# The first pair of an attention kernel: k and q as float32 through the SyncE queue, rounded on the chip, and the head ordered by hand

## The chip, the cores and the metric

The kernel runs on one core of one Trainium2 chip. The metric is the device time of one execution in microseconds (us). A run of the kernel is one execution; a figure for a kernel is the median of its fast runs. The span of a trace is about 1.7 us shorter than the time of the same execution (206.9 us for 208.6 us in the kernel before).

## The reference

Attention with a choice of chunks, followed by a gated MLP. Cut to what matters:

```python
# q, k, v: (4, 8, 768, 64) float32; chunk = 32, 24 chunks, top_k = 6
k_min = np.min(k_chunks, axis=3); k_max = np.max(k_chunks, axis=3)
ub = np.sum(np.maximum(q * k_min, q * k_max), axis=-1)      # a bound for each query and chunk
ub = np.where(causal, ub, -1e9)
top_chunks = np.argsort(ub, axis=-1)[..., -top_k:]
scores = scale * q @ k.T, masked to the chosen chunks and to the causal triangle
attn = exp(scores - max) / sum;  out = attn @ v
# then the MLP on (4, 768, 512): h = relu(x @ w_in); u, v = halves of h
# v normalised, v_s = w_spatial @ v + b;  result = (u * v_s) @ w_out, float32
```

## The kernel before

The 32 heads are taken as 16 pairs. Each pair goes through the same steps: transposes of k on TensorE (`k_transpose`), the chunk maxima and minima on DVE (`k_max`, `k_min`), transposes of q and its positive and negative parts (`q_transpose`, `q_parts`), bound matmuls (`bounds`), the six best chunks (`top`, `select`), and then for each head six score matmuls, an exponential on ACT for each, and value matmuls (`scores`, `values`). At about 55 us the matmuls of the MLP begin; they are mixed in and fill TensorE's gaps.

```python
        def k_bounds(self):                      # "km": the small operand of the bound matmuls
            for hi, (d0, d1) in enumerate(HALF):
                copy = nc.gpsimd.tensor_copy if 2 <= self.i < 4 else nc.scalar.copy
                ...
        def k_operand(self, hi):                 # "kh": the score operand
            copy = nc.scalar.copy if self.i < 1 else nc.vector.tensor_copy
            ...
        def a_copy(self, hi):
            copy = nc.vector.tensor_copy if self.i < 2 and hi == 0 else nc.scalar.copy
            ...
        def triangle(self, hi):
            if self.b == 0:                      # none for the first four pairs
                return
            ...
            nc.gpsimd.affine_select(out=blk, in_=blk, compare_op=Alu.is_ge, fill=0.0, ...)
```

Loads change float32 to float16 on the way. The Trainium skill ("DMA: Bandwidth & Descriptors", section "SWDGE vs HWDGE vs iDMA") says that a DMA that casts has to be issued from GpSimd, which the profile calls POOL. So all loads of before are POOL instructions.

```python
    def load_k(g, hi, xy=None):
        ...
            nc.gpsimd.dma_start(out=t[:, xy, :, 1 - hi, :], in_=source(k, b, h + xy, 1))
    def load_w_out(j):
        nc.gpsimd.dma_start(out=w_out_sb[:, j], in_=moe_w_out[j * P:(j + 1) * P, :])
```

The program is written as a list of steps with a "beat" each (`at(beat, step)`), issued in order of beats. What is issued so is then still reordered, engine by engine, by a scheduler that works from its own estimates. Only what stands inside `manual_schedule` stays in the written order; in before that is TensorE alone, up to beat 6:

```python
    at(B0, load_k, 0, 0, 0)                      # B0 = -30: the head
    ...
    at(B0, init_ring, 0)                         # zeros in the first of three q buffers, on DVE
    ...
    for j in range(KO):
        at(76 + 6 * j, load_w_out, j)
    ...
    with tc.manual_schedule(engines={mybir.EngineType.PE}):
        for beat in sorted(b for b in beats if b < 6):
            for fn, args in beats.pop(beat):
                fn(*args)
    for beat in sorted(beats):                   # the scheduler orders all engines here
        for fn, args in beats[beat]:
            fn(*args)
```

The softmax here doesn't subtract the row's maximum and nothing guards it: scores larger than these inputs give would overflow.

Of the kernel before, what the change touches and what calls it, by code (L numbers as in the profile page):

```python
# [10 lines left out]
F32 = mybir.dt.float32  # L11
# [5 lines left out]
P = 128  # L17
# [31 lines left out]
def kernel(  # L49
# [46 lines left out]
    def at(beat, fn, *args):  # L96
        beats[beat].append((fn, args))
# [12 lines left out]
    later = cp.tile([P, (NQT - 1) * 2 * NCH], F16)  # L110
    expand = cp.tile([D, S], F16)
    eps_t = cp.tile([P, 1], F32)

    def init_identity():
        nc.vector.memset(identity, 0.0)
# [2 lines left out]

    def init_ring(i):

        nc.vector.memset(qs_ring[i][:, :, :, 0:4:3, :], 0.0)

    def init_small():
        nc.vector.memset(km_ring[0], 0.0)
        nc.vector.memset(km_ring[1], 0.0)
        nc.vector.memset(eps_t, 1e-6)
        for t in v_ring:
            nc.vector.memset(t[:, :, :, D:D + 2], 1.0)

    def init_expand():  # L130

# [5 lines left out]

    def init_masks():

        nc.gpsimd.memset(later, 0.0)  # L140
        lv = later.rearrange("p (t h c) -> p t h c", h=2, c=NCH)
        nc.gpsimd.affine_select(out=lv, in_=lv, compare_op=Alu.is_ge, fill=NEG, base=CPT,
                                channel_multiplier=1, pattern=[[CPT, NQT - 1], [0, 2], [-1, NCH]])
        nc.gpsimd.memset(tri, 0.0)
        nc.gpsimd.affine_select(out=tri, in_=tri, compare_op=Alu.is_ge, fill=NEG,
                                base=0, channel_multiplier=-1, pattern=[[1, P]])

    def init_kh(i):
        for hi, (d0, d1) in enumerate(HALF):
            nc.scalar.copy(kh_ring[i][hi][d0:d1, :], expand)  # L150


    W = 2 * NCH
# [3 lines left out]
    class Pair:  # L157
# [26 lines left out]

        def k_bounds(self):
            for hi, (d0, d1) in enumerate(HALF):
                copy = nc.gpsimd.tensor_copy if 2 <= self.i < 4 else nc.scalar.copy
                s0, s1 = HALF[1 - hi]
                copy(self.km[d0:d1, :, hi], self.kmm[s0:s1])

# [10 lines left out]

        def q_transpose(self):
            self.tr = self.trans_tile()
            for t in range(1, NQT):
                nc.tensor.transpose(self.tr[:, t * P:(t + 1) * P], self.qs[:, t, 1:3, :], identity)  # L205

        def q_parts(self, m):
            if m == 0:
                self.rq = sb.tile([P, 2, S], F16, tag="rq", name="rq")
                nc.vector.tensor_scalar(self.rq[:, 0, P:S], in0=self.tr[:, P:S], scalar1=0.0, scalar2=None, op0=Alu.max)  # L210
            elif self.i < 1:
                nc.scalar.activation(self.rq[:, 1, P:S], self.tr[:, P:S], func=Act.Relu, scale=-1.0)
            else:
                nc.vector.tensor_scalar(self.rq[:, 1, P:S], in0=self.tr[:, P:S], scalar1=-1.0, scalar2=0.0,
                                        op0=Alu.mult, op1=Alu.max)
# [37 lines left out]
        def a_copy(self, hi):  # L253
            if self.i >= 8:
                return
            copy = nc.vector.tensor_copy if self.i < 2 and hi == 0 else nc.scalar.copy
            copy(self.a[:, :, hi, :], self.tr.rearrange("d (t s) -> d t s", s=P))  # L257


# [55 lines left out]
    def source(x, b, h, n):  # L315
        return x[b, h:h + n].rearrange("h (so si) d -> si (h so) d", si=P)

    def load_k(g, hi, xy=None):
        b, hp = divmod(2 * g, HP)
        if ("k", g) not in tiles:  # L320
            tiles["k", g] = sb.tile([P, 2, NQT, 2, D], F16, tag="k", name="k", bufs=3)
        t = tiles["k", g]
        for x in range(2):
            pairs[2 * g + x].k = t[:, x]
        h = 2 * hp + 2 * hi
        if xy is None:
            nc.gpsimd.dma_start(out=t[:, :, :, 1 - hi, :].rearrange("p x t d -> p (x t) d"), in_=source(k, b, h, 2))  # L327
        else:
            nc.gpsimd.dma_start(out=t[:, xy, :, 1 - hi, :], in_=source(k, b, h + xy, 1))

    def load_q(g, hi, xy=None):
        b, hp = divmod(2 * g, HP)
        t = qs_ring[g % 3][:, :, :, 1 + hi, :]
        h = 2 * hp + 2 * hi
        if xy is None:
            nc.gpsimd.dma_start(out=t.rearrange("p x t d -> p (x t) d"), in_=source(q, b, h, 2))  # L336
        else:
            nc.gpsimd.dma_start(out=t[:, xy], in_=source(q, b, h + xy, 1))

    def load_v(g):  # L340
        b, hp = divmod(2 * g, HP)
        t = v_ring[g % 3]
        nc.gpsimd.dma_start(out=t.rearrange("p h t c -> p (h t) c")[:, :, 0:D], in_=source(v, b, 2 * hp, 4))
        for x in range(2):
            pairs[2 * g + x].v = [t[:, x], t[:, x + 2]]

# [7 lines left out]
    def load_w_in(j):  # L354
        for hi in range(2):
            r = (4 * (j // 2) + j % 2 + 2 * hi) * D
            nc.gpsimd.dma_start(out=w_in_sb[hi * D:(hi + 1) * D, j], in_=moe_w_in[r:r + D, :])

    def load_w_spatial(j):
        nc.gpsimd.dma_start(out=ws_raw[:, j], in_=moe_w_spatial[j * P:(j + 1) * P, :])  # L360
# [90 lines left out]

    B0 = -30
    pairs = [Pair(i) for i in range(NPAIR)]
    at(B0, load_k, 0, 0, 0)
    at(B0, load_k, 0, 1, 0)
    at(B0, init_identity)
    at(B0, load_q, 0, 0, 0)
    at(B0, load_q, 0, 1, 0)
    at(B0, init_ring, 0)
    at(B0, init_small)  # L460
    at(B0, init_expand)
    at(B0, load_k, 0, 0, 1)
    at(B0, load_k, 0, 1, 1)
    at(B0, init_masks)
    at(B0, load_q, 0, 0, 1)
    at(B0, load_q, 0, 1, 1)
    at(B0, load_v, 0)
    at(B0, init_ring, 1)
    at(B0, init_ring, 2)
    at(B0, init_kh, 0)  # L470
    at(B0, init_kh, 1)
    at(40, load_b)
    for g in range(1, NPAIR // 2):
        t0 = 2 * g * BEATS
        for hi in range(2):
            at(t0 - 40 + hi, load_k, g, hi)
            at(t0 - 36 + hi, load_q, g, hi)
        at(t0 - 18, load_v, g)
    for i, p in enumerate(pairs):
        t0 = i * BEATS  # L480
        for hi in range(2):
            for g in range(len(TILES)):
                at(t0 + 6 * hi + g, p.scores, hi, g)
            at(t0 + 6 * hi + 6, p.triangle, hi)
            at(t0 + 6 * hi + 6, p.values, hi, LOWER[0], True)
            at(t0 + 6 * hi + 8, p.values, hi, LOWER[1])
            at(t0 + 6 * hi + 10, p.values, hi, DIAG, False, True)
            at(t0 + 6 * hi + 11, p.normalise, hi)
        at(t0 + 18, p.x_transpose)
    for i, p in enumerate(pairs):  # L490
        t0 = i * BEATS
        if i < 2:
            continue
        t0 += 4 if i < 4 else 0
        at(t0 - (22 if i < 4 else 27), p.k_transpose)
        at(t0 - 22, p.k_max)
        at(t0 - 21, p.q_transpose)
        at(t0 - 20, p.k_min)
        at(t0 - 19, p.q_parts, 0)
        at(t0 - 18, p.q_parts, 1)  # L500
        at(t0 - 17, p.k_bounds)
        at(t0 - 16, p.bounds)
        at(t0 - 15, p.k_operand, 0)
        at(t0 - 14, p.top, 0)
        at(t0 - 13, p.top, 1)
        at(t0 - 12, p.select)
        at(t0 - 11, p.k_operand, 1)
        at(t0 - 10, p.a_transpose, 0)
        at(t0 - 9, p.a_copy, 0)
        at(t0 - 7, p.a_transpose, 1)  # L510
        at(t0 - 6, p.a_copy, 1)
    p, n = pairs[0:2]
    for beat, *step in (
            (B0 + 1, p.k_transpose), (B0 + 1, p.k_max), (B0 + 1, p.k_min), (B0 + 1, p.k_operand, 0),
            (B0 + 1, p.q_transpose), (B0 + 1, p.q_parts, 0), (B0 + 1, p.k_bounds),
            (B0 + 1, p.q_parts, 1), (B0 + 1, p.k_operand, 1), (B0 + 1, p.bounds), (B0 + 1, p.top, 0),
            (B0 + 1, p.top, 1), (B0 + 1, p.select), (B0 + 1, init_kh, 2), (B0 + 1, init_kh, 3), (B0 + 1, p.a_transpose, 0), (B0 + 1, p.a_copy, 0),
            (B0 + 1, n.k_transpose), (B0 + 1, p.a_transpose, 1), (B0 + 1, n.k_max), (B0 + 1, p.a_copy, 1), (B0 + 1, n.k_min),
            (B0 + 1, n.k_operand, 0),
            (0, n.q_transpose), (1, n.q_parts, 0), (1, n.k_bounds), (1, n.q_parts, 1),  # L520
            (1, n.k_operand, 1), (2, n.bounds), (3, n.top, 0), (3, n.top, 1), (4, n.select), (5, n.a_transpose, 0),
            (5, n.a_copy, 0), (6, n.a_transpose, 1), (6, n.a_copy, 1)):
        at(beat, *step)
    for j in range(NDO):
        at(20 + 8 * j, load_w_in, j)
# [30 lines left out]
            at(first + done * count // total, fn)  # L556
            done += cost

    with tc.manual_schedule(engines={mybir.EngineType.PE}):
        for beat in sorted(b for b in beats if b < 6):  # L560
            for fn, args in beats.pop(beat):
                fn(*args)
    for beat in sorted(beats):
# [31 lines left out]
```

## Time and profile before

| | before |
|---|---|
| median, lowest, highest of 3 runs | 209.1, 208.97, 209.35 us |
| span of the profiled run (208.6 us) | 206.9 us |
| first k transpose, first k maximum | 5.75, 6.58 us |
| first exponential | 15.29 us |
| "landmark" on ACT (below) | 51.28 us |
| first triangular mask | 52.93 to 53.79 us |
| idle TensorE in the first 60 us | 14.2 us |

The page of before gives busy time by engine, and the span in 40 slices (a digit is the busy share in tenths). TensorE (PE) is at 90% or more from the twelfth slice (57 us) to the last but one, so only the first 60 us have anything to give.

```profile
PE 187.8 (91%) x1922; PEld 115.1 (56%) x1922; DVE 154.5 (75%) x454; ACT 158.1 (76%) x326; POOL 80.5 (39%) x100
...
PE   0368999898899999999999999999999999999992
```

The table of busy time by stretch says the same in numbers; each line is a stretch, its length, then the busy time of each engine with its number of instructions. The busy times of PE in the first eight of the ten stretches asked for add up to 45.8 of 60 us.

```profile
core 0: us, PE busy (x) PEld busy (x) DVE busy (x) ACT busy (x) POOL busy (x), PEclk, DMA share, GB/s
0.00:6.00 6.00, 0.25 (x3) 0.28 (x4) 3.34 (x12) 3.10 (x4) 4.81 (x10) 1.00 0.73 46
6.00:10.00 4.00, 1.60 (x13) 0.94 (x10) 2.31 (x3) 2.94 (x6) 4.00 (x9) 1.00 1.34 86
...
50.00:60.00 10.00, 9.12 (x122) 6.42 (x121) 8.63 (x28) 9.41 (x22) 9.28 (x12) 1.00 2.10 170
60.00:80.00 20.00, 19.39 (x233) 12.85 (x231) 18.99 (x60) 17.45 (x37) 10.72 (x11) 1.00 1.98 130
80.00:200.00 120.00, 119.62 (x1054) 66.98 (x1053) 87.27 (x237) 86.28 (x184) 20.38 (x22) 1.00 0.82 120
```

The chain of waits in the head of before (start, length, what): the k load takes 3.33 us from issue to landing, the two reductions follow, and then ACT does kh, km and the negative part of q (`rq`) one after the other, from 8.50 to 10.52. That is 2.7 us between the end of the minimum (8.42) and the end of the bound matmuls (11.13).

```profile
2.28 3.33 DMA k<-in_k_dram
...
5.75 0.81 PE kTp L170 x6
...
6.58 0.96 DVE kmm L178
7.54 0.88 DVE kmm L182
...
8.50 0.79 ACT kh L194
...
9.81 0.71 ACT rq L212
...
10.57 0.56 PE ub L222 x9
```

### The profile page before, as it was taken

The numbers are of one execution on the slowest core, as the hardware profiler recorded it, in microseconds if no ns is written. First come the engines' busy times: TensorE is split into PE (matmuls) and PEld (weight loads), VectorE is DVE, ScalarE is ACT, GpSimd is POOL, SyncE is SP. The second block draws the span as 40 slices with busy tenths as digits, with TensorE's granted clock in tenths as the row PEclk, the third lists the DMA queues.
The fourth block names the chain that finished last, engine by engine and source line by source line (L and its number), as shares of the span: only waits on it lengthen the run. The fifth ranks groups of instructions, "written<-read, shape, count | busy, mean of one in ns | idle before, by whom it ended". The sixth has DMA issues, their size and how long they took to land.

```text
span 206.9 us, 5068 instructions
## 1 busy us (share of the span) xinstructions
PE 187.8 (91%) x1922; PEld 115.1 (56%) x1922; DVE 154.5 (75%) x454; ACT 158.1 (76%) x326; POOL 80.5 (39%) x100
## 2 busy tenths in 40 slices
PE   0368999898899999999999999999999999999992
PEld 0266776775666665656655656565555454444440
DVE  6467979989799989899797999887647456365520
ACT  4797989899998889785989996669999830666042
POOL 7997659596992463236114111111111110000000
PEclk9999999999999999999999999999999999999999
DMA  5999999999999999979998926648782124540356
GB/s 38 92 118 154 140 178 158 173 177 167 177 162 162 97 119 128 135 130 147 149 278 153 180 62 57 127 88 158 181 166 65 38 29 92 187 152 3 72 128 256
DMA packets 114424, 27.27 MB, mean 132 GB/s; under 512 B 109536, under 2 KB 110816, under 8 KB 114400
## 3 DMA queue, kind: packets, MB, share of 16 engines
q0 software_dynamic: 76544, 12.20, 89.8%
q1 hardware_dynamic: 37856, 14.75, 36.4%
q8 instruction: 15, 0.25, 0.5%
q14 instruction: 9, 0.07, 0.1%
HBM read 24.38 MB, written 6.29 MB: 148 GB/s over the span
## 4 chain that ended last, share of the span: by engine, by line
PE 69%; ACT 17%; DVE 8%; issue 2%; DMA 2%; POOL 0%; DVEq 0%; ACTq 0%; POOLq 0%
PE mlp L388 40%; PE sc L266 12%; ACT e L271 10%; PE acc L289 7%; PE kTp L170 2%; ACT a L257 2%; DVE kmm L178 2%; PE ub L222 2%; DMA k<-in_k_dram 2%; PE trm L251 2%; ACT vraw L398 1%; PE tr L205 1%; DVE vn L412 1%; DVE kmm L182 1%; ACT u L420 1%
## 5 line engine op out<-in xcount | busy, mean ns | idle before, releaser
L271 ACT ACTIVATE e<-sc 128x512 f16<-128x512 f32 x192 | 96.9, 553 | 14.8 <-PE sc L266 13.4
L266 PE MATMUL sc<-a,kh 128*128 128x512 f16 (+3 forms) x256 | 65.5, 308 | 2.1 <-ACT e L271 1.5
L388 PE MATMUL mlp<-w_in_sb,xT 128*128 128x512 f16 x192 | 53.0, 379 | 0.1
L278 POOL TENSOR_SCALAR_AFFINE_SELECT e<-e 128x768 f16<-128x768 f16 x24 | 20.9, 869 | 66.3 <-ACT e L271 66.3
L289 PEld LDWEIGHTS <-e 128*128 128x128 f16 x672 | 31.4, 97 | 17.0 <-DVE x L297 3.8
L388 PE MATMUL mlp<-vn,wsT 128*128 128x512 f16 x144 | 37.3, 379 | 0.0
L289 PE MATMUL acc<-vt,e 128*128 128x65 f16 x672 | 35.3, 193 | 0.7 <-DVE x L297 0.4
L266 PEld LDWEIGHTS <-kh 128*128 128x128 f16 x256 | 22.7, 98 | 13.3 <-issue 0.8
L437 ACT COPY o<-mlp 128x512 f32<-128x512 f32 x24 | 14.1, 586 | 19.5 <-PE mlp L388 19.1
L400 DVE BATCH_NORM_STATS2 stats<-vraw 128x6 f32<-128x512 f32 x24 | 16.6, 693 | 12.9 <-ACT vraw L398 12.5
L388 PE MATMUL mlp<-w_out_sb,gT 128*128 128x512 f16 x96 | 25.1, 379 | 0.0
L388 PEld LDWEIGHTS <-xT 128*128 128x128 f16 x192 | 17.2, 97 | 12.6 <-issue 0.4
L427 DVE SCALAR_TENSOR_TENSOR g<-mlp,b_col,u 128x512 f16<-128x512 f32 x24 | 17.9, 748 | 7.3 <-PE mlp L388 6.2
L232 DVE MAX8 max<-ub 128x8 f32<-128x8 f32 (+4 forms) x160 | 15.6, 165 | 5.1 <-PE ub L222 4.9
L388 PEld LDWEIGHTS <-wsT 128*128 128x128 f16 x144 | 12.9, 98 | 10.4
L178 DVE TENSOR_REDUCE kmm<-kTp 128x24 f16<-128x768 f16 x16 | 15.2, 948 | 3.7 <-PE kTp L170 2.7
L297 DVE TENSOR_TENSOR x<-acc,rec 128x384 f16<-128x384 f32 x32 | 17.6, 551 | 0.4
L336 POOL DMA_DIRECT2D qs<-in_q_dram x14 | 14.6, 1049 | 5.9 <-PE sc L266 5.9
L194 DVE COPY kh<-kTp 64x768 f16<-64x768 f16 x30 | 16.5, 549 | 0.5
L398 ACT ACTIVATE vraw<-mlp 128x512 f32<-128x512 f32 x24 | 14.4, 601 | 3.0 <-PE mlp L388 3.0
L420 ACT ACTIVATE u<-mlp 128x512 f16<-128x512 f32 x24 | 14.3, 598 | 1.7 <-PE mlp L388 1.5
L327 POOL DMA_DIRECT2D k<-in_k_dram x14 | 14.4, 1045 | 2.5 <-PE kTp L170 1.8
(67 smaller groups left out, 230.2 us busy)
## 6 DMA issues: line engine op xcount, KB each, us to landing
out_dram<-o SPq DMA_DIRECT2D x24, 256.0 KB, 2.3
vt<-in_v_dram POOLq DMA_DIRECT2D x8, 384.0 KB, 8.8
k<-in_k_dram POOLq DMA_DIRECT2D x14, 192.0 KB, 8.1
qs<-in_q_dram POOLq DMA_DIRECT2D x14, 192.0 KB, 7.5
ws_raw<-in_moe_w_spatial_dram POOLq DMA_DIRECT2D x6, 192.0 KB, 6.9
w_in_sb<-in_moe_w_in_dram POOLq DMA_DIRECT2D x8, 128.0 KB, 6.9
w_out_sb<-in_moe_w_out_dram POOLq DMA_DIRECT2D x4, 128.0 KB, 7.9
k<-in_k_dram POOLq DMA_DIRECT2D x4, 96.0 KB, 3.4
```

The lines of the kernel that those rows point to most:

```text
L178: nc.vector.tensor_reduce(self.kmm[:, 0, :], self.kT.rearrange("d (c ch) -> d c ch", ch=CHUNK), axis=AX.X, op=Alu.max)
L194: copy(self.kh[hi][d0:d1], self.kT[d0:d1])
L266: mm(sc[:, col:col + n], lhsT=self.kh[hi][:, t * P:(t + 1) * P], rhs=self.a[:, q0 // P:(q0 + n) // P, hi, :], start=True, stop=not diag)
L271: nc.scalar.activation(out=self.e[hi][:, g * 512:g * 512 + width], in_=sc[:, 0:width], func=Act.Exp, scale=scale)
L278: nc.gpsimd.affine_select(out=blk, in_=blk, compare_op=Alu.is_ge, fill=0.0, base=0, channel_multiplier=-1, pattern=[[0, NQT], [1, P]])
L289: mm(self.av[:, qi, :], lhsT=self.e[hi][:, c:c + P], rhs=self.v[hi][:, t, 0:D + 1], start=first and n == 0, stop=last and n == len(blocks) ...
L297: nc.vector.tensor_tensor(self.x16[:, :, hi, :], in0=self.av[:, :, 0:D], in1=rec.to_broadcast([P, NQT, D]), op=Alu.mult)
L388: mm(st[group][:, 0:cols], lhsT=lhsT, rhs=rhs, start=(j == 0), stop=(j == n - 1))
L398: nc.scalar.activation(st["vraw"][:, ti, :], h, func=Act.Relu)
L400: nc.vector.bn_stats(stats, st["vraw"][:, ti, :])
L420: nc.scalar.activation(st["u"][:, ti, :], h, func=Act.Relu)
L427: nc.vector.scalar_tensor_tensor(g, in0=vs, scalar=b_col[:, ti:ti + 1], in1=st["u"][:, ti, :], op0=Alu.add, op1=Alu.mult)
```

## The change

The intent: get the first pair's k and q sooner by plain float32 copies on the SyncE (SP) queue and round them on DVE (k) and ACT (q); shorten the head's chain by a better order and a better split between ACT and DVE; and fix that order for TensorE, DVE and ACT up to beat 7. To make room on DVE, two of the three buffer memsets go to POOL, and the POOL loads of the first three groups and of w_in are kept in program order. The loads of w_spatial, w_out and the bias are not.

```diff
-        nc.vector.memset(qs_ring[i][:, :, :, 0:4:3, :], 0.0)
+        (nc.vector if i == 0 else nc.gpsimd).memset(qs_ring[i][:, :, :, 0:4:3, :], 0.0)
...
-                copy = nc.gpsimd.tensor_copy if 2 <= self.i < 4 else nc.scalar.copy      # km
+                copy = nc.gpsimd.tensor_copy if 2 <= self.i < 2 else nc.scalar.copy
...
-            elif self.i < 1:                                                             # rq
-                nc.scalar.activation(self.rq[:, 1, P:S], self.tr[:, P:S], func=Act.Relu, scale=-1.0)
             else:
                 nc.vector.tensor_scalar(self.rq[:, 1, P:S], ...)
...
-            copy = nc.vector.tensor_copy if self.i < 2 and hi == 0 else nc.scalar.copy   # a
+            copy = nc.vector.tensor_copy if self.i < 1 and hi == 0 else nc.scalar.copy
...
+    def load(now, **kw):
+        ins = nc.gpsimd.dma_start(**kw)
+        if now:
+            tc.keep_in_program_order(ins)
...
+    def load_first():
+        for x, t in ((k, k_first), (q, q_first)):
+            for hi in range(2):
+                nc.sync.dma_start(out=t[:, hi if x is q else 1 - hi], in_=...)
+
+    def round_first(what):
+        if what == "k":
+            nc.vector.tensor_copy(tiles["k", 0][:, 0], k_first.rearrange("p h t d -> p t h d"))
+        else:
+            nc.scalar.copy(pairs[0].qs[:, :, 1:3, :], q_first.rearrange("p h t d -> p t h d"))
...
+        (B0, load_first), (B0, init_identity), (B0, init_ring, 0), (B0, init_expand), ...
+        (B0, init_kh, 0, 0, nc.scalar), ...          # three fills on ACT
+        (B0, init_kh, 1, 1, nc.vector), ...          # five fills on DVE
+        (B0, round_first, "k"), (B0, round_first, "q"),
+        (B0, p.k_transpose), (B0, p.k_max), (B0, p.k_min), (B0, p.q_transpose), (B0, p.q_parts, 0),
+        (B0, p.k_bounds), (B0, p.q_parts, 1), (B0, p.bounds), (B0, p.k_operand, 0), ...
...
-    with tc.manual_schedule(engines={mybir.EngineType.PE}):
-        for beat in sorted(b for b in beats if b < 6):
+    with tc.manual_schedule(engines={mybir.EngineType.PE,mybir.EngineType.DVE,mybir.EngineType.Activation}):
+        for beat in sorted(b for b in beats if b < 7):
```

Cut: the same pinning in the other loads, the beats of pairs 1 to 3, which are written anew, and `later` and `tri` cleared on DVE in place of POOL.

## The prediction

> **What bounds the kernel.** The page gives PE 91% of 206.9 us, ACT 76%, DVE 75%. A table by stretch of time splits this: PE is 98 to 100% busy from 60 to 200 us, so nothing there can be gained by reordering the head. Its 14 us of idle in the first 60 us are the only stake: 5.8 us before 6 us (first matmul at 5.75, when the first k landed), 2.4 in 6-10, 1.9 in 10-15, then about 4 over 15-60. From the first exponential (15.29 us, timeline) to 60 us ACT is the limit: 41.0 of 44.7 us busy, against PE near 90%.
>
> **Removed from the head's chain** (chain of waits, durations read there). After the k minimum ends (8.42) ACT does kh 0.79, km 0.46, the negative relu 0.71 in series, and the bound matmuls end at 11.13. With the relu on DVE (0.40) and the kh copies after km, they could end about 1.95 us after the minimum: a saving of 0.8 to 1.3 us. The next pair's k transposes (0.64) leave the path between select and first score and go into the shadow of the max8s; but both a transposes now precede the score (0.7 of them behind the 0.56 DVE copy). Net about 0.2 to 0.4 saved. Five kh fills leave ACT, but it was waiting then.
>
> **Added.** Four float32 loads on SP. The trace's SP copies take about 0.5 us of queue each, so k can be issued by about 1.8 and, with the 3.3 us landing of before, be there near 4.5 to 5.5. This gains nothing unless DVE is free: DVE now has, in order, ring memset, expand, sub_chunk, small memsets, five kh fills and the k rounding. From 0.49 for a 64x768 expand I estimate 0.25 to 0.35 per fill and 0.45 to 0.85 for the rounding. The k maximum, 6.58 before, then starts at 6.3 to 7.2. Worse: POOL starts a 1536-element memset just when identity is ready (estimate 1.4 us, from 0.26 us for 128 and 0.36 for 240 elements). The Trainium skill (SBUF — State Buffer, Who interferes with whom) says that a DVE copy in a two-port mode and a POOL operation block each other fully. The trace may already show it: sub_chunk, 128x128, took 0.51 us beside POOL's DMA issues. Expand could wait 1 us.
>
> **Moved onto the ACT stage:** a copy of pair 1 (0.80) and the km copies of pairs 2 and 3 (0.48 each, on POOL before): 1.76 us in the stage ACT bounds. Against this the fixed order should reclaim perhaps 1 to 2 of its 3.7 us idle, as pair 1's selection comes some 2 us earlier.
>
> **Sum.** First exponential earlier by about 1 us (range -0.8 to +2.5), ACT load +1.76, idle -1 to -2.5. I expect 1.6 us gained: **207.5 us, 8 in 10 between 205.0 and 209.5**. Chances: faster by over 2% 0.12, within 2% 0.85, slower 0.03.
>
> **What would show it.** Right: first exponential at 14 to 14.7; k maximum at 6.3 to 7.2, released by PE or DVE work and not by the load; bounds done about 2 us after the k minimum; PE idle of the first 60 us down to about 12.6; 60 to 200 us unchanged. The POOL lock: expand starting, or lasting, 1 us beyond the identity select. Loads too slow: k rounding waits on its DMA after 6 us.
>
> **What would make it wrong.** k maximum well before 6 us with PE fed continuously from 12 us: then 204 to 205. Rigid order of ACT and DVE making one late item hold all behind it, or the extra ACT copies not absorbed: 209 to 210. PE clock: 128x512 matmuls cost 0.63 us until about 17 us and 0.38 after.

## More of the kernel before

From the fifth pair on, a triangular mask on POOL (`triangle`) has to run on a head's exponentials before the first value matmuls of that head may start.

The landmark is a place that can be found in every trace of this study: the last time before 60 us that ACT does two km copies (0.47 us together), then one exponential, then one copy `a`. It cuts the time in three: up to the first exponential, from there to the landmark, and from the landmark to the end of the span.

POOL's timeline of before around the first triangular mask (L278 is the mask).

The order is two k loads, the mask, a v load, a w_out load.

```profile
50.84 2.04 POOL L327 DMA_DIRECT2D k<-in_k_dram  x2 [0.67 <-PE sc L266]
52.93 0.86 POOL L278 TENSOR_SCALAR_AFFINE_SELECT e<-e 128x768 f16<-128x768 f16 x1
53.74 1.43 POOL L343 DMA_DIRECT2D vt<-in_v_dram  x1
55.17 0.56 POOL L363 DMA_DIRECT2D w_out_sb<-in_moe_w_out_dram  x1
```

## The result, and the profile after

Ratios in this document are the mean time of one kernel's fast runs over that of the other's fast runs of the same rounds, with a 95% interval, so they are not quite the ratio of the medians that are quoted.

| | before | after |
|---|---|---|
| median (lowest to highest, 4 runs each) | 209.22 us (208.97 to 209.35) | 210.25 us (209.73 to 210.41) |
| ratio | | 1.0047 (1.0026 to 1.0067) |
| span of the profiled run | 206.9 us | 208.6 us |
| first k maximum, end of k minimum | 6.58, 8.42 us | 8.59, 10.41 us |
| end of minimum to end of bounds | 2.71 us | 1.41 us |
| first exponential | 15.29 us | 15.35 us |
| first exponential to landmark | 35.99 us | 36.23 us |
| landmark to end of span | 155.6 us | 157.0 us |
| idle PE in the first 60 us | 14.2 us | 16.4 us |

The change made the kernel a little slower, by 0.5%. The two profiled runs differ by 1.7 us, more than the medians (1.0), because the profiled run of before was a fast one; by thirds the 1.7 us are 0.06 + 0.24 + 1.4.

The page and the table by stretch of after, to be compared with those of before: PE's busy times in 60:80 and 80:200 are the same to 0.15 us, the first 6 us hold no matmul at all, and in 50:60 PE is busy 7.52 us in place of 9.12.

```profile
PE 187.7 (90%) x1922; PEld 114.9 (55%) x1922; DVE 157.2 (75%) x460; ACT 155.8 (75%) x326; POOL 78.6 (38%) x92
...
PE   0278899998599999999999999999999999999992
```

```profile
core 0: us, PE busy (x) PEld busy (x) DVE busy (x) ACT busy (x) POOL busy (x), PEclk, DMA share, GB/s
0.00:6.00 6.00, 0.00 (x0) 0.00 (x0) 4.22 (x16) 2.99 (x4) 4.63 (x10) 1.00 0.61 131
6.00:10.00 4.00, 1.55 (x12) 1.20 (x12) 3.04 (x5) 1.52 (x2) 4.00 (x5) 1.00 1.16 74
...
50.00:60.00 10.00, 7.52 (x109) 5.09 (x106) 7.15 (x24) 7.68 (x18) 8.17 (x10) 1.00 1.90 178
60.00:80.00 20.00, 19.38 (x234) 13.16 (x231) 18.88 (x62) 17.54 (x39) 10.08 (x11) 1.00 1.73 113
80.00:200.00 120.00, 119.77 (x1068) 67.24 (x1067) 88.89 (x241) 87.23 (x185) 21.93 (x24) 1.00 0.90 120
```

The head first. The chain of waits of after no longer goes through the load. It goes through POOL (a memset and the identity) and then through DVE alone: `expand` takes 1.70 us where it took 0.49, the small memsets and five kh fills follow, and the rounding of k starts at 6.93 only.

```profile
2.21 0.30 POOL identity L118
...
2.54 1.70 DVE expand L135
...
6.93 0.75 DVE k L356
...
7.73 0.84 PE kTp L174 x6
...
8.59 0.96 DVE kmm L182
...
10.81 0.41 DVE rq L216
...
11.27 0.55 PE ub L224 x9
```

For comparison, `expand` in DVE's timeline of before, where no POOL memset ran beside it:

```profile
3.64 0.49 DVE L132 TENSOR_SCALAR expand<-identity 64x768 f16<-64x768 f16 x1
```

So k is worked on 2 us later than before, and the reordered chain behind it is 1.9 us shorter (4.94 us from the end of the minimum to the first exponential, before 6.87). The two cancel.

Then the stretch at 50 us. POOL's timeline of after: between the two k loads and the first triangular mask (now L280) three w_out loads have moved in, and the second of them waited 1.20 us for a q load to land. The mask starts at 55.18; before it started at 52.93.

```profile
50.31 2.04 POOL L321 DMA_DIRECT2D k<-in_k_dram  x2 [0.76 <-PE acc L291]
52.34 0.57 POOL L383 DMA_DIRECT2D w_out_sb<-in_moe_w_out_dram  x1
54.11 1.07 POOL L383 DMA_DIRECT2D w_out_sb<-in_moe_w_out_dram  x2 [1.20 <-DMA qs<-in_q_dram]
55.18 0.88 POOL L280 TENSOR_SCALAR_AFFINE_SELECT e<-e 128x768 f16<-128x768 f16 x1
```

Why a w_out load should wait for a q load: in the built program POOL's loads take eight semaphores in turn (106 to 113 in the trace's operands), and each issue waits until the load that used its semaphore last has landed. Counted back in the timeline, the eighth issue before the w_out load of 54.11 is the q load of 44.80. The chain of waits shows it, with 9.03 us from issue to landing, then the mask and the value matmuls (`acc`) that need it:

```profile
44.80 9.03 DMA qs<-in_q_dram
...
54.11 1.07 POOL w_out_sb L383 x2
55.18 0.89 POOL e L280
...
56.12 0.36 PE acc L291 x6
```

TensorE waits 1.6 us there, a wait that before does not have, and ACT, which needs TensorE's next scores, is idle 2.21 us before its exponential at 56.73; in before the same exponential came at 54.66 after 0.44 us. The lag of after behind before is 0.30 us at the landmark and 2.07 us at this exponential.

### The profile page after: what moved, and what is told of

Same layout as the page of the kernel before. It is cut to its first block, busy times and chain, and to the rows that moved or that the text cites. A ratio compares the mean times of both kernels' runs of the same rounds, so it can differ in the third digit from the quotient of the medians.

```text
span 208.6 us, 5070 instructions
## 1 busy us (share of the span) xinstructions
PE 187.7 (90%) x1922; PEld 114.9 (55%) x1922; DVE 157.2 (75%) x460; ACT 155.8 (75%) x326; POOL 78.6 (38%) x92
## 3 DMA queue, kind: packets, MB, share of 16 engines
HBM read 24.38 MB, written 6.29 MB: 147 GB/s over the span
## 4 chain that ended last, share of the span: by engine, by line
PE 64%; ACT 18%; DVE 7%; DMA 4%; POOL 3%; issue 2%; POOLq 0%
PE mlp L408 40%; PE sc L268 11%; ACT e L273 10%; PE acc L291 6%; DMA qs<-in_q_dram 4%; ACT a L259 3%; PE kTp L174 2%; PE ub L224 2%; ACT vraw L418 1%; DVE vn L432 1%; PE tr L210 1%; ACT u L440 1%; PE trm L253 1%; ACT km L193 1%; POOL k L321 1%
## 5 line engine op out<-in xcount | busy, mean ns | idle before, releaser
L280 POOL TENSOR_SCALAR_AFFINE_SELECT e<-e 128x768 f16<-128x768 f16 x24 | 20.8, 868 | 67.1 <-ACT e L273 67.1
L420 DVE BATCH_NORM_STATS2 stats<-vraw 128x6 f32<-128x512 f32 x24 | 16.6, 693 | 12.9 <-ACT vraw L418 12.6
L408 PEld LDWEIGHTS <-xT 128*128 128x128 f16 x192 | 17.2, 97 | 12.6 <-issue 0.4
L321 POOL DMA_DIRECT2D qs<-in_q_dram x16 | 16.2, 1025 | 6.0 <-PE sc L268 3.2
L321 POOL DMA_DIRECT2D k<-in_k_dram x16 | 16.3, 1032 | 2.5 <-PE kTp L174 1.8
```

The costliest lines, as they stand in the source:

```text
L321: ins = nc.gpsimd.dma_start(**kw)
L408: mm(st[group][:, 0:cols], lhsT=lhsT, rhs=rhs, start=(j == 0), stop=(j == n - 1))
L420: nc.vector.bn_stats(stats, st["vraw"][:, ti, :])
```

## The experiments

My theory after reading the two traces: the loss is POOL's order. The change left the w_out loads to the scheduler while it pinned others; three of them came to stand ahead of the first mask. It is not in the diff as an intention at all. A second part of the theory, for the gain that did not come: the memset on POOL that runs beside `expand` blocks it, and everything behind on DVE is late (the lock).

The rivals: the copies moved onto ACT (1.76 us of work) cost what was lost (B in the expectations); and the fills on DVE, or the float32 loads themselves, make the head late, k's or q's load landing too late to be of use (Q in the expectations is the part about q).

Labels: a_ is the kernel after with edits, b_ is before with edits, p_ is after with the w_out loads kept in program order and further edits. The kernels were sent in three lots, and each is compared with the runs of before of its own lot (medians 208.84, 208.63, 208.63 us). All gave correct results.

### a_pin: all weight loads in program order

```diff
-        nc.gpsimd.dma_start(out=ws_raw[:, j], in_=moe_w_spatial[j * P:(j + 1) * P, :])
+        load(True, out=ws_raw[:, j], in_=moe_w_spatial[j * P:(j + 1) * P, :])
-        nc.gpsimd.dma_start(out=w_out_sb[:, j], in_=moe_w_out[j * P:(j + 1) * P, :])
+        load(True, out=w_out_sb[:, j], in_=moe_w_out[j * P:(j + 1) * P, :])
-        nc.gpsimd.dma_start(out=b_col, in_=...)
+        load(True, out=b_col, in_=...)
```

> Changed kernel; only the order of POOL's load issues from about 40 us on differs: the weight loads stay behind what was traced before them, so one w_out load instead of three stands between the k loads and the first triangular mask. PE, DVE, ACT and SP orders are identical. Theory A (the loss is the 1.6 us PE wait for that mask, behind loads that wait for the landing of earlier loads): the mask is done by 53.8 to 54.3 us instead of 56.06, PE's wait for it vanishes, time falls by 1.4 to 1.9 us, to about 208.6, thus slightly faster than before. Rival B (the loss is ACT work moved into the stage that ACT bounds) and rival C (the late first k maximum, 8.59 instead of 6.58): the time stays at 210.0 to 210.4, as both are untouched.

Measured: 213.4 us (212.61 to 214.8), ratio 1.0229 (1.020 to 1.0258). The mask ends at 51.99 and the wait for it is gone: PE is busy 9.12 us in 50:60, exactly as in before. But a new wait has come. A load of w_spatial now stands behind the second mask; it is issued at 56.02, and TensorE waits for it. The first line is from the list of what PE waited for between 50 and 80 us (total, times, longest), the second from POOL's timeline, both of a_pin.

```profile
PE wtr L388 <- DMA ws_raw<-in_moe_w_spatial_dram: 2.5, 1, 2.5
```

```profile
56.02 0.57 POOL L321 DMA_DIRECT2D ws_raw<-in_moe_w_spatial_dram  x1
```

In the 60 to 80 us stretch PE was busy 16.99 us, at a granted clock of 0.91: from 63.82 us on the column reads 0.50 for 3.41 us, which I estimate to cost 1.7 us at half speed. With the wait of 2.5 us this makes up the 4.0 us by which the time from landmark to end exceeds 155.2 (table at the end of this section). So the edit took away the wait that it was to take away and put a larger one, and a stretch at half clock, in its place: the theory's mechanism was seen, the time says nothing against or for it. Keeping everything in program order is no repair if the written order is not good.

The half clock did not follow every wait. a_pin_nolock (wait of 3.3 us) and p_act (2.6 us) have such a stretch too; a_pin_late12 has a longer wait, 3.5 us, and none. Counted in steps of 3.41 us from the moment at which TensorE reached full speed (see p_ctl2), the three dips each follow a step in which PE was idle for 2.5 to 3.1 us; in a_pin_late12 the wait fell across two steps with 1.8 us idle in each, and in after and b_wA no step at the wait has more than 1.6. That is as far as these six traces go.

### a_pin_nolock and a_pin_late12: the same, with POOL's memsets later

a_pin_nolock is a_pin with the third buffer's memset kept in its place in the program, behind POOL's loads of the first two groups; a_pin_late12 does so with both memsets.

```diff
-        (nc.vector if i == 0 else nc.gpsimd).memset(qs_ring[i][:, :, :, 0:4:3, :], 0.0)
+        ins = (nc.vector if i == 0 else nc.gpsimd).memset(qs_ring[i][:, :, :, 0:4:3, :], 0.0)
+        if i in (2,):                  # a_pin_late12: (1, 2), and memset 1 asked for at beat -10
+            tc.keep_in_program_order(ins)
```

> As a_pin, and the second ring memset of POOL (1.38 us) stands behind the loads of the first two groups instead of just behind the identity. Theory L (that memset holds expand back: 1.70 us instead of the 0.49 of before): expand takes about 0.5 us, everything up to the first exponential comes 1.2 us earlier (first k maximum 7.4, first exponential 14.15). If the stage after the head passes an earlier start on, the time falls by 0.8 to 1.2 against a_pin. Rival (what expand waited for is something else, or the gain is swallowed by ACT later): expand stays at 1.7, or the first exponential is earlier and the time moves by under 0.3.

> As a_pin_nolock, and POOL's first ring memset (1.38 us, ahead of the identity) also stands behind the loads. The identity is then ready near 1.4 instead of 2.5, DVE's own ring memset ends at 1.8, expand starts near 1.9. DVE reaches the k rounding near 5.1; k landed by about 4.6 in the changed kernel, so the first k maximum should be at 6.7 and the first exponential at 13.5. Time against a_pin: -1.5 to -1.9 if the head passes on, under -0.5 if ACT swallows it. Rival (k comes later than that): DVE's rounding waits for the load.

Measured: 212.05 us, ratio 1.0133 (1.0096 to 1.0169; one run of six, 213.35, counts as slow and is left out), and 210.39 us, ratio 1.0080 (1.0059 to 1.0101). The wait for w_spatial is in both (3.3 and 3.5 us). The head is what counts here. Without the memset beside it, `expand` takes 0.55 us, the k maximum starts at 7.45 and the first exponential at 14.20: 1.15 us earlier than in after (DVE's timeline of a_pin_nolock below). With both memsets out of the way `expand` starts at 1.73, the k maximum at 6.57, and the first exponential at 13.33, 2.02 us earlier. The landmark moves by as much against after (50.43 and 49.55 against 51.58): what the head gains is passed on one to one. That the memset lengthens `expand` is shown, and its cost is 1.15 us; POOL's other memset, which holds the identity back, costs another 0.9.

```profile
2.54 0.55 DVE L137 TENSOR_SCALAR expand<-identity 64x768 f16<-64x768 f16 x1 [0.73 <-POOL identity L118]
```

### b_wA: the kernel before with only its w_out loads moved

```diff
-        at(76 + 6 * j, load_w_out, j)
+        at(76 + j, load_w_out, j)
```

> The kernel before, with one number changed so that four w_out loads instead of one stand ahead of the k loads and of the first triangular mask on POOL; all other engines' orders are identical. Theory A: the k load behind them waits for the landing of the q load eight issues earlier (about 54 us), the mask is done near 56 instead of 53.8, PE waits for it about 1.8 us and the time rises by 1.4 to 2.2, to about 211. Rivals B and C: unchanged, 209.0 to 209.5.

Measured: 211.67 us (210.65 to 212.92), ratio 1.0133 (1.0101 to 1.0165). Only the order on POOL differs from before: all four w_out loads ahead of the k loads and the mask. The first exponential (15.26) and the landmark (51.31) are those of before. Then the mask runs at 55.74, and the list of PE's waits between 50 and 62 us has the new wait of after, larger:

```profile
PE acc L289 <- POOL e L278: 2.4, 1, 2.4
```

This is the cause alone, put into the kernel that did not have it: 2.8 us lost in the median, with nothing else of the change in it.

### p_ctl and p_ctl2: the change with only its w_out loads in program order

```diff
-        nc.gpsimd.dma_start(out=w_out_sb[:, j], in_=moe_w_out[j * P:(j + 1) * P, :])
+        load(True, out=w_out_sb[:, j], in_=moe_w_out[j * P:(j + 1) * P, :])
```

This is the reverse test. Against after, only places of w_out loads on POOL differ: one, in place of three, stands between the k loads and the first mask. It was run in two lots because the profiled run of the first was at a clock of 0.577 (327.74 us) and so gave no trace to compare.

> The changed kernel with only the w_out loads kept in the order in which the program asks for them; the w_spatial loads, which the first attempt (a_pin) also held back and which then kept PE waiting 2.5 us, are left alone. One w_out load instead of three stands before the first triangular mask; all other engines' orders are those of the changed kernel. Theory A: PE's 1.6 us wait for the mask vanishes, no new load wait appears, and the time is 208.2 to 209.0 where the changed kernel had 210.25. Rivals B (extra ACT work) and C (late head): 210.0 to 210.5.

> The kernel of p_ctl once more, whose profiled execution fell in a slow one (clock 0.58), so that its trace could not be read. Theory A: first exponential at 15.35 and the landmark of the ACT stage near 51.6 to 52.2 as in the changed kernel, first triangular mask done by 54, no PE wait for POOL's mask or for w_spatial, time 208.5 to 209.2. Rival (the wait only moved): another PE wait of over 1 us after 50 us.

Measured: 208.73 us (four fast runs of five), ratio 1.0002 (0.9986 to 1.0018), and 208.82 us, ratio 1.0022 (0.9996 to 1.0048). So the loss of after against before (1.0047) is gone, or nearly: the rest of the change neither gains nor loses. That includes the copies moved onto ACT and the late head, which are both still in p_ctl: neither rival made the loss. In the trace of p_ctl2 no wait for the mask is left, and the time from landmark to end is 155.2 us, against 157.0 in after and 155.6 in before.

The runs of p_ctl2 fall in two groups: 208.51, 208.75, 208.51, 208.89, and 209.93, 210.16. The profiled one is of the slower group, and its trace shows where: the stretch from first exponential to landmark took 37.66 us in place of 36.23. TensorE changed to its faster pace later. The third set of k transposes, in p_ctl2 and then in after (PE's timelines):

```profile
20.33 0.85 PE L174 MATMUL kTp<-identity,k 128*128 128x128 f16 x6
```

```profile
19.31 0.50 PE L174 MATMUL kTp<-identity,k 128*128 128x128 f16 x6
```

The same six matmuls took 0.85 us at 20.3 in one and 0.50 at 19.3 in the other; before 16 us they take 0.8 in all traces. The granted clock column cannot show this: it reads 1.00 throughout, because the trace's clock record (in trace.npz) begins only with the step to full speed and the time before counts as 1.00. Counted from the start of the span, the record puts that step at 16.34 us in after and at 21.20 us in p_ctl2. The later it came after the first exponential, the longer was the stretch to the landmark: 36.0 to 36.4 us where it came within 3.0 us (p_act, with its late km copy, left out), 36.84 at 4.1 us (a_pin), 37.66 and 37.62 at 5.9 us (p_ctl2, p_late_a). More on this in the last section. The 210.16 run has no trace, so that its cause is the same is likely and not shown.

### p_lock and p_late: POOL's order mended with care, and its memsets late

p_lock is p_ctl with the bias and w_spatial loads in program order too, the last two w_spatial loads asked for earlier so that none falls behind a mask, and the third buffer's memset late. p_late puts the second buffer's memset late as well.

```diff
+        if i in (2,):                  # p_late: (1, 2), and memset 1 asked for at beat -10
+            tc.keep_in_program_order(ins)
-        at(44 + 4 * j, load_w_spatial, j)
+        at(44 + 4 * j if j < 4 else 54 + j, load_w_spatial, j)
```

> As p_ctl, with POOL's second ring memset behind the loads (and all loads kept in program order, without the late w_spatial load of a_pin_nolock). There the profile showed expand at 0.55 instead of 1.70 us, the first exponential at 14.20 instead of 15.35, and a landmark of the ACT stage at 50.43 instead of 51.58: the head's gain was passed on whole. Expected: 0.9 to 1.3 us below p_ctl, about 207.4. Rival: swallowed later, under 0.3 below p_ctl.

> As p_lock, with POOL's first ring memset also behind the loads. First exponential at 13.3, landmark at 49.6 as a_pin_late12 had them. Expected: 1.8 to 2.2 us below p_ctl, about 206.4, which beats both the kernel before and the changed kernel. Rival: another queue item takes the gain back, as the late w_spatial load did (its PE wait was 3.5 us there).

Measured: p_lock 207.49 us, ratio 0.9947 (0.9931 to 0.9963); p_late 206.54 us, ratio 0.9913 (0.9889 to 0.9937). p_late beats both kernels, by 2.1 us in the median against before. Its POOL timeline has the mask right behind a k load and its v and w_out loads behind the mask:

```profile
47.91 1.03 POOL L323 DMA_DIRECT2D k<-in_k_dram  x1
48.92 0.90 POOL L282 TENSOR_SCALAR_AFFINE_SELECT e<-e 128x768 f16<-128x768 f16 x1
49.74 1.45 POOL L323 DMA_DIRECT2D vt<-in_v_dram  x1
51.16 0.58 POOL L323 DMA_DIRECT2D w_out_sb<-in_moe_w_out_dram  x1
```

The first exponential is at 14.20 and 13.32, as in the a_pin pair, and this time the end moves along: 205.8 and 204.8 us of span.

### p_act: the copies given back by ACT

```diff
-                copy = nc.gpsimd.tensor_copy if 2 <= self.i < 2 else nc.scalar.copy
+                copy = nc.gpsimd.tensor_copy if 2 <= self.i < 4 else nc.scalar.copy
-            copy = nc.vector.tensor_copy if self.i < 1 and hi == 0 else nc.scalar.copy
+            copy = nc.vector.tensor_copy if self.i < 2 and hi == 0 else nc.scalar.copy
```

This is p_ctl with the 1.76 us of copies back on DVE and POOL, as in before: the rival B put to the test.

> As p_ctl, with the 1.76 us of work that the change moved onto ACT put back: the first a copy of pair 1 on DVE and the km copies of pairs 2 and 3 on POOL. Theory A' (the fixed order absorbed that work: from first exponential to the landmark took 35.99 us before and 36.23 after): within 0.6 us of p_ctl. Rival B: 1.2 to 1.8 us below p_ctl.

Measured: 211.52 us, ratio 1.0139 (1.0099 to 1.018): slower by more than 2 us than p_ctl, not faster. The list of PE's waits in the first 60 us says why:

```profile
PE ub L224 <- POOL km L193: 2.6, 1, 2.6
```

A km copy on POOL now waits in a pinned row of loads (it starts at 33.56), and the bound matmuls wait for it. As placed here, the km copies had to leave POOL once its loads were pinned. For the rival this run is no clean test: the edit brought a wait and a stretch at half clock (34.46 to 37.88 us) of its own, and the scheduler also ordered matmuls otherwise. What speaks against the rival is p_ctl, which has all of the copies on ACT and does not lose.

### p_late_a: only the copy of pair 1 given back

```diff
-            copy = nc.vector.tensor_copy if self.i < 1 and hi == 0 else nc.scalar.copy
+            copy = nc.vector.tensor_copy if self.i < 2 and hi == 0 else nc.scalar.copy
```

This is p_late with that one edit, which takes 0.8 us from ACT. (The scheduler also ordered some matmuls and one DVE copy otherwise, between 18 and 31 us; POOL's order is the same.)

> As p_late, with only pair 1's first a copy (0.80 us on ACT) back on DVE; POOL's order is that of p_late, so this is the clean test of the extra ACT work that p_act was not (there the km copies on POOL stood behind loads and PE waited 2.6 us for one). If ACT's extra 0.80 us is on the chain: 0.5 to 0.9 us below p_late, about 205.8. If absorbed: within 0.3 of p_late, 206.5.

Measured: 206.95 us, ratio 0.9929 (0.9905 to 0.9954), against 206.54 and 0.9913 of p_late. It was run at another time. No gain: 0.8 us less on ACT is worth nothing that shows. (The profiled run, 208.52 us, had the late pace of TensorE again.) So this copy was absorbed, and the rival falls for it. No run takes only the km copies (0.96 us) off ACT.

### p_fill: the five fills moved from DVE to ACT

```diff
-        (B0, init_kh, 1, 1, nc.vector),
-        (B0, init_kh, 2, 0, nc.vector),
-        ...                                     # three more on DVE
+        (B0, init_kh, 1, 1, nc.scalar),
+        (B0, init_kh, 2, 0, nc.scalar),
         (B0, round_first, "k"),
...
         (B0, p.k_operand, 1),
+        ...                                     # the other three on ACT, here
```

The other edits are those of p_late. It asks whether the fills in front of k's rounding cost anything.

> As p_late, with the five kh fills that the change put on DVE back on ACT, in its idle stretches before the q rounding and after the kh copies. DVE can then round k as soon as it lands, after 3.2 us. Theory Q (the q load and its rounding on ACT bound the head now, 6.66 to 7.49 in a_pin_late12): first k maximum 0.2 to 0.6 earlier than 6.57, but the first exponential within 0.3 of 13.33 and the time within 0.4 of p_late. Rival (DVE's queue bounds it): first exponential 0.5 to 1.0 earlier.

Measured: 207.05 us, ratio 0.9929 (0.9910 to 0.9947): no gain over p_late. It also tells when the loads land. DVE, now free early, waits for k until 4.79 us; ACT waits for q until 6.76 (timelines of DVE, then ACT, of p_fill):

```profile
4.79 0.58 DVE L358 CAST k<-k_first 128x768 f16<-128x768 f32 x1 [1.94 <-DMA k_first<-in_k_dram]
```

```profile
6.76 0.83 ACT L360 CAST qs<-q_first 128x768 f16<-128x768 f32 x1 [0.32 <-DMA q_first<-in_q_dram]
```

The k maximum starts 0.28 us earlier than in p_late (6.29 against 6.57), but q is rounded 0.32 us later than there (6.76 against 6.44), the q transposes wait 1.4 us for it, and DVE waits for them after the k minimum; the first exponential is at 13.43 against 13.32. So in p_late the fills on DVE cost nothing that shows: with k earlier by 0.28 us, q is the next limit of the head.

### b_sp: the kernel before with only the float32 loads

`load_first` and `round_first` of the change put into before, nothing else, with the scheduler's own order on DVE and ACT.

```diff
-    at(B0, load_k, 0, 0, 0)
-    at(B0, load_k, 0, 1, 0)
+    at(B0, load_first)
...
-    at(B0, load_q, 0, 0, 0)
-    at(B0, load_q, 0, 1, 0)
...
+    at(B0, round_first, "k")
+    at(B0, round_first, "q")
```

> The kernel before with the float32 loads of the first pair by SP and their rounding alone, none of the ordering by hand. The order chosen automatically puts ACT's q rounding ahead of four kh fills (0.84 each) and those ahead of the km copies, so a q that lands at 6.2 puts km near 11.5 (9.3 before). Expected: first exponential 2 to 3 us later than 15.29, time 210.5 to 212. If instead the earlier load alone pays, as the change's intent has it: first exponential before 15 and time under 208.9.

Measured: 211.86 us, ratio 1.0152 (1.0134 to 1.0169). The first exponential comes at 18.64, 3.35 us later than in before. The rounding of q stands first on ACT and waits for its load to 7.75, and all fills and the km copies stand behind it (ACT's timeline):

```profile
7.75 0.83 ACT L352 CAST qs<-q_first 128x768 f16<-128x768 f32 x1 [5.66 <-DMA q_first<-in_q_dram]
8.49 3.35 ACT L152 COPY kh<-expand 64x768 f16<-64x768 f16 x4
```

So the load by SP alone is no gain: with the scheduler's order it costs 3 us. (Here, too, several w_out loads stand before the mask, which ends at 57.03, but the landmark is at 54.76 by then and nothing waits for it.)

### All traces by thirds

Times in us, from ACT's timeline and the spans.

| | first exponential | to landmark | landmark to end |
|---|---|---|---|
| before | 15.29 | 35.99 | 155.6 |
| after | 15.35 | 36.23 | 157.0 |
| b_wA | 15.26 | 36.05 | 158.6 |
| a_pin | 15.35 | 36.84 | 159.2 |
| a_pin_nolock | 14.20 | 36.23 | 160.1 |
| a_pin_late12 | 13.33 | 36.22 | 158.7 |
| p_ctl2 (late TensorE pace) | 15.35 | 37.66 | 155.2 |
| p_lock | 14.20 | 36.32 | 155.3 |
| p_late | 13.32 | 36.23 | 155.3 |
| p_late_a (late TensorE pace) | 13.45 | 37.62 | 155.7 |
| p_fill | 13.43 | 36.37 | 155.3 |
| p_act | 15.35 | 39.64 | 155.2 |
| b_sp | 18.64 | 36.12 | 155.2 |

The last third is 155.2 to 155.7 us in each kernel without a wait of TensorE for POOL's mask or for w_spatial behind the landmark, and 157.0 to 160.1 in each that has one.

## Why the prediction was right or wrong

The predicted 207.5 us (205.0 to 209.5) is not what came: 210.25 us, above the range, though inside the class "within 2%" that was given 0.85.

- **The failed step is the term "idle -1 to -2.5" of the sum**, "the fixed order should reclaim perhaps 1 to 2 of its 3.7 us idle", and with it "PE idle of the first 60 us down to about 12.6". Up to the landmark the term came as forecast: between the first exponential and the landmark ACT's idle time fell by 2.06 us, from 3.46 (busy 32.53 of 35.99) to 1.40 (busy 34.83 of 36.23). Just behind it most of that was lost: ACT stood idle 2.21 us where it had been 0.44. Over the whole stage to 60 us its idle time fell by 0.33 us only (4.01 to 3.68), and PE's in the first 60 us rose from 14.2 to 16.4. The path that the prediction lacked is POOL's. The hand order was set for TensorE, DVE and ACT; POOL was left out of my account, and POOL is where the scheduler, with some loads pinned and others free, put three w_out loads ahead of the first mask. That made a wait of 1.6 us on TensorE at 54 to 56 us, and the time from landmark to end 1.4 us longer. b_wA shows this cause alone (+2.8 us with four loads), and p_ctl shows the change without it (1.0002).
- **"First exponential earlier by about 1 us": it came 0.06 later.** The term was mis-sized through its first part. "The k maximum, 6.58 before, then starts at 6.3 to 7.2" measured 8.59. I had named the reason ("Expand could wait 1 us") and not put it into the centre; it measured 1.15 us (a_pin_nolock). The Trainium skill ("SBUF — State Buffer", section "Who interferes with whom") says that a DVE instruction in a two-port mode and a GpSimd one exclude each other for the whole instruction. The trace agrees: `expand` beside the memset lasted 1.70 us and ended 0.41 us after the memset's end (4.24 against 3.83); without it, 0.55. (That `expand` runs in such a mode no view tells. `sub_chunk`, named as a first sign, took 0.20 us in after with POOL idle beside it, against 0.51, which fits.) A further 0.9 us is the other memset ahead of the identity on POOL (p_late against p_lock), which I had not counted at all. The five fills took 0.41 us each (2.03 in all), over the estimate of 0.25 to 0.35.
- **The shorter chain was right.** "Bounds done about 2 us after the k minimum" measured 1.41, before 2.71; from minimum to first exponential 1.93 us were saved. This gain is real, and p_late shows it at the end of the span.
- **The loads were right.** "There near 4.5 to 5.5": k landed at 4.79, as p_fill shows, and "this gains nothing unless DVE is free" is what after shows. It went further than I thought: in p_late, where DVE starts the rounding at 4.91, soon after k has landed, the k maximum starts at 6.57, in before at 6.58. The earlier landing is used up by the rounding, so what p_late gains in the head (1.97 us at the first exponential) comes from the order behind it, and not from the float32 loads. (No run has the hand order with the old loads, so this is read from the traces and not tried.) That q lands later (ACT's wait for it ended between 6.17 and 6.78 in the traces with the hand order that show one) and is the next limit, I did not say.
- **"1.76 us in the stage ACT bounds" came, and was offset.** From first exponential to landmark ACT was busy 2.30 us longer (34.83 against 32.53) and idle 2.06 us less, so after needed only 0.24 us more than before. Taking 0.8 us of it back gained nothing (p_late_a), and giving the km copies to POOL cost 2.6 us of waiting (p_act).
- **"60 to 200 us unchanged" was right** by the table: 139.01 us of PE busy in it before, 139.15 after (the sums of the last two stretches shown). The lost time lay just in front of it.
- **Of the named ways to be wrong**, "rigid order of ACT and DVE making one late item hold all behind it" comes near: rigid order did it, but the order of POOL, and not by intent. What I had called the result of that, "209 to 210", is close to what came.

What stays open: the part of POOL's order in the small rest. p_ctl and p_ctl2 differ by 0.2% with intervals that overlap, so that the rest of the change is worth nothing is known to about 0.4%, not better.

## What to carry to other kernels

When a part of an engine's instructions is pinned and the rest left to a scheduler, look at what moves in that engine's whole stream, also far behind the part that was changed: a load is cheap itself, but ahead of work that others wait for it brings its own wait along. Small work moved to a "free" engine has to be checked against what runs beside it (the memset that lengthened `expand`) and what stands behind it (the identity). And cut the trace at landmarks that every variant has: thirds of the span told here at once which part of the change an experiment touched, where the total time did not.

## What the Trainium skill lacked or had wrong

- "TensorE: Matmul & The Clock Gate" ("Part 1: The HAM clock gate") says that the array runs at half rate until about 3.4 us of sustained work, in a free-running window, so that the number of slow matmuls varies between runs, at under 1% of a typical span. The trace agrees that there are two paces (0.62 to 0.63 us, then 0.38, for a 128x512 matmul; these durations are not in the ratio of two). What the page lacks is the size in a kernel with a thin head: the change came at 16.34 us in after and at 21.20 us in p_ctl2, of nearly the same program, with a granted clock of 1.00 in the profile's column in both, and the later one had its landmark 1.43 us later (0.7% of the span), as much as the effect that was being measured.
- "SBUF — State Buffer" ("Who interferes with whom") was right in kind for the case: 1.70 us against 0.55. It has no case of a chain that is held up by it, where the lengthened DVE instruction costs all behind it its full 1.15 us.
- "VectorE: DVE Perf Modes" ("Zero memsets can be issued as uint32 (trn2)") says that a memset costs one cycle for each element, so that zeros are better written as 4-byte words. The runs agree (on DVE 0.16 us for 120 uint32 elements, 0.70 us for 768), and add what it does not say: the same memset given to POOL came as 1536 float16 elements and took 1.38 us, on DVE as 768 uint32 elements, half of that.
- "DMA: Bandwidth & Descriptors" ("Anatomy of one DMA — SWDGE (gpsimd) path") gives about 2.0 us and the bytes over 436 GB/s for one DMA. By that a 192 KB load would take an estimated 2.5 us; the q load that held POOL here took 9.03 us with many others under way, and the median of such loads in after was 7.6 us. The page has a passage on small descriptors, but no time for a load of them with many others under way.
- No page that I used tells of the wait that the eighth load before puts on a load's issue (1.20 us on POOL in after). It comes from how the program was built, and it is what turned three cheap instructions into a late mask.
